# Loading Q and K of two batches in runs of eight rows by head pair, with a fixed order of the first loads, in a fused attention and feed-forward kernel

## The chip, the cores and the metric

The kernel runs on one core of one Trainium2 chip. The metric is the device time of one execution in microseconds (us). A profiled execution gives a span that is 1.7 to 2.2 us shorter than the time of the same execution.

TensorE (PE in the profile) does the matmuls; its weight loads are listed as PEld. ScalarE is ACT, VectorE is DVE, GpSimd is POOL and SyncE is SP. The granted TensorE clock is printed as PEclk, in shares of full speed.

## The reference

The inputs are float32. Batch B is 8, heads H are 8, sequence S is 576 and head width D is 64. After attention, 4,608 tokens go through a feed-forward layer, 512 to 2,048 to 512.

```python
scores = (1 / sqrt(D)) * (q @ k.transpose(0, 1, 3, 2))
mask = abs(pos[:, None] - pos[None, :]) <= 32          # a band of 32 rows on each side
scores = where(mask, scores, -1e9)
attn = exp(scores - max(scores)); attn = attn / (sum(attn) + 1e-9)
x = (attn @ v).transpose(0, 2, 1, 3).reshape(B * S, H * D)
h = x @ w_in
out = (s * maximum(h, 0) ** 2 + b) @ w_out
```

## The kernel before

The kernel is one list of tasks. Every task has an engine, an estimated cost and a priority `key`; a planner simulates the engines with these costs and fixes the order on each engine. A wrong cost gives a wrong order, because the engines execute what the planner chose.

Batches 0 and 1 are transposed by TensorE, batches 2 to 7 by DMA. For the first two, a chunk of 128 pairs of rows is loaded, cast to bf16, transposed and evicted:

```python
# batches 0 and 1, before: rows in pairs (i = 2), so a run in memory is 2 * 64 floats = 512 bytes
def pairs_chunk(b, name, t0, n, key, load_key, banks, slack=0.0):
    ...
    add("sp", lambda e: e.dma_start(
        STG[si][0:n, 0:1024].rearrange("p (h c) -> p h c", h=H),
        src_of[name][b, :, t0:t0 + 2 * n, :].rearrange("h (p i) d -> p h (i d)", i=2)), ...)
    # cast STG -> NAT on ACT, POOL or DVE; eight transposes on PE
    # Q: two evictions to QT on ACT; K: four evictions to KBD on DVE and ACT
```

A transposed query block has its columns sorted by row parity: first all even rows, then all odd rows. The scores in PSUM have that order too. The exponential puts them back into natural order while it writes bf16 to SBUF, with step 2 inside a row of 128.

```python
def unit(b, m):                                   # two key tiles of 64 keys, all 4 head pairs
    ...
    rhs = QT[slot][:, :, pr, lo // 2:hi // 2]     # for the scores of one tile and head pair
    ...                                           # b < 2: a matmul with MASKB adds the band first
    src = src.rearrange("p a (i c) -> p a i c", i=2)
    add("act", lambda e, src=src, dst=dst: e.activation(
        dst.rearrange("p a (c i) -> p a i c", i=2), src, AF.Exp, bias=0.0, scale=0.125),
        190 + 0.833 * 4 * w, ...)                 # the planner's cost: no term for the step
    # then attention times V, reciprocal, scaling (DVE), 4 transposes (PE), eviction to XT (ACT)
```

A batch has nine tiles and hence nine exponentials, seven of 512 columns and two of 384. The order of loads and attention, cut:

```python
qk(0, 0, 128); qk(0, 256, 128)        # Q and K of batch 0, rows 0-255 and 256-511
V of batch 0 (8 loads); qk(0, 512, 32); cast_v(0); units (0, 0) to (0, 4)
w_in (8 loads); w_out, first half
qk(1, 0, 128); V of batch 1; unit(1, 0)
qk(1, 256, 128); unit(1, 1); unit(1, 2); qk(1, 512, 32)
w_out, second half; unit(1, 3); unit(1, 4)
# batches 2 to 7 with PACE and PACEV: after which unit of the batch before their loads may start
```

The feed-forward layers run on token blocks of 128, 128, 256 and then 512. "First layer" is `w<-xt,win`, "second layer" is `o<-wout,gt`. The first block of 512 tokens is called block 3 below.

The softmax here doesn't subtract the row's maximum and nothing guards it: scores larger than these inputs give would overflow.

## Time and profile before

| What | Before | View |
|---|---|---|
| time, median of 3 runs | 332.48 us (332.16 to 333.7) | times |
| span; TensorE busy | 331.1 us; 308.5 us | page |
| first score matmul | 10.70 us | timeline |
| first first-layer matmul | 24.20 us | timeline |
| first 512-column first-layer matmul (block 3) | 74.98 us | timeline |
| one exponential, 512 columns / 384 columns | 0.74 / 0.60 us | groups by shape |

The first view is the page of the kernel before. Parts of the page are separated by dots. The rows of digits cut the span into 40 equal slices; a digit is the busy share, or the granted clock, in tenths (9 is 90% or more). The line that starts with "PE o" is the chain of work that ended last, as shares by line. The last line is a group: busy time, mean ns of one, then the idle time of the engine before them and what ended it.

```profile
span 331.1 us, 5839 instructions
...
PE 308.5 (93%) x2199; PEld 179.5 (54%) x2234; DVE 206.6 (62%) x485; ACT 166.4 (50%) x270; POOL 87.6 (26%) x136
...
PE   1778998899999999999989999999999999999995
...
PEclk9999999799999999999999999999999999999999
...
PE o L717 31%; PE w L698 29%; PE avn L582 6%; SPq L432 5%; DMA vst<-in_v_dram 5%; PE sc L543 3%; DMA stg<-in_moe_w_in_dram 3%; DMA stg<-in_moe_w_out_dram 3%; POOL vst L432 2%; SPq L456 2%; DMA out_dram<-outs 2%; ACT vbd L445 1%; SPq L416 1%; PE o L740 1%; DVE vbd L446 0%
...
L560 ACT ACTIVATE exo<-sc 128x512 bf16<-128x512 f32 x32 | 23.8, 743 | 4.8 <-PE sc L543 4.6
```

TensorE is busy 93% of the span and is idle mainly in the first three slices.

The second view is the table of stretches of the kernel before. The columns are named in the first line; "(x)" stands for a count of instructions. DMA share is the mean busy share of the 16 DMA engines; values above 1 occur, and only comparisons are drawn from it.

```profile
core 0: us, PE busy (x) PEld busy (x) DVE busy (x) ACT busy (x) POOL busy (x), PEclk, DMA share, GB/s
10.00:20.00 10.00, 7.43 (x64) 5.32 (x66) 5.02 (x8) 8.18 (x13) 6.24 (x7) 1.00 1.24 252
20.00:30.00 10.00, 7.60 (x130) 6.82 (x128) 6.13 (x14) 7.71 (x15) 3.85 (x4) 1.00 1.06 373
30.00:40.00 10.00, 10.00 (x126) 9.23 (x124) 6.82 (x14) 5.15 (x9) 3.33 (x3) 1.00 1.13 313
70.00:80.00 10.00, 8.84 (x79) 5.83 (x78) 8.20 (x19) 6.66 (x11) 0.00 (x0) 1.00 0.95 202
```

In steps of 10 us ScalarE is never full: 8.18 us is its highest value here. In steps of 2 us it is: 1.89 to 1.98 us of 2 in each step from 14 to 24 us. TensorE is idle 2.6 us of 10 to 20 us and 2.4 us of 20 to 30 us.

The third view is the timeline of ScalarE in the kernel before, with start and duration in us.

```profile
16.55 0.72 ACT L560 ACTIVATE exo<-sc 128x512 bf16<-128x512 f32 x1
17.38 0.75 ACT L560 ACTIVATE exe<-sc 128x512 bf16<-128x512 f32 x1
18.15 1.04 ACT L445 CAST vbd<-vst 64x1024 bf16<-64x1024 f32 x1
```

One exponential takes about 0.74 us, a cast of V 1.04 us.

The fourth view is one line of TensorE's timeline before, the first score. The brackets give the idle time before it and what ended it.

```profile
10.70 0.48 PE L549 MATMUL sc<-maskb,ident 128*128 128x384 bf16 x1 [1.49 <-DVE kbd L491]
```

The fifth is the table of stretches before for 2.5 to 10 us, where Q, K and V of batch 0 arrive. The last two numbers are the DMA share and GB/s. The clock before them is no proof of full speed at the front: it reads 1.00 here, where eight transposes of 128 columns take 1.03 us, against 0.61 us at 40 us.

```profile
2.50:10.00 7.50, 2.07 (x16) 1.54 (x16) 5.67 (x20) 4.60 (x6) 6.36 (x18) 1.00 1.15 291
```

The sixth is the list of waits of TensorE before: total us, times, longest.

```profile
PE w L473 <- ACT nat L465: 6.1, 1, 6.1
...
PE sc L543 <- ACT exe L560: 1.1, 1, 1.1
```

### The profile page before, as it was taken

To read this page: it belongs to the slowest core of one execution; us is meant where nothing else is said; L and a number is where in the kernel's file an instruction comes from. 1 tells how busy PE (TensorE), PEld (TensorE's weight loads), DVE (VectorE), ACT (ScalarE), POOL (GpSimd) and SP (SyncE) were. 2 spreads that over 40 slices of the span, in tenths; PEclk is the share of its full clock that TensorE was granted. 3 is DMA by queue.
4 is the path that set the end of the run, shared out by engine and by line. 5 is a ranking of instruction groups with operands and counts; after the bars stand their busy time and mean duration, and the time that the engine had idled before them with its cause. 6 is when DMAs were issued, how large, how long until landed. Compare 5 with 4: busy or idle time off the path is not lost.

```text
span 331.1 us, 5839 instructions
## 1 busy us (share of the span) xinstructions
PE 308.5 (93%) x2199; PEld 179.5 (54%) x2234; DVE 206.6 (62%) x485; ACT 166.4 (50%) x270; POOL 87.6 (26%) x136
## 2 busy tenths in 40 slices
PE   1778998899999999999989999999999999999995
PEld 1567996775554555456445555555455544444442
DVE  6556564269777776898578768765874453323411
ACT  6696497229552664657175655444644433333300
POOL 8562443830910226044205500450000000000000
PEclk9999999799999999999999999999999999999999
DMA  8999999899999699979998996999811111000021
GB/s 211 224 363 357 295 195 297 219 241 167 209 202 197 193 195 206 230 170 245 173 228 163 225 212 145 247 169 213 146 56 54 56 46 62 35 32 34 32 93 68
DMA packets 107836, 57.15 MB, mean 173 GB/s; under 512 B 56608, under 2 KB 100128, under 8 KB 107808
## 3 DMA queue, kind: packets, MB, share of 16 engines
q1 hardware_dynamic: 103200, 49.69, 68.7%
q0 software_dynamic: 4608, 7.08, 11.3%
q8 instruction: 17, 0.28, 0.4%
q14 instruction: 11, 0.09, 0.1%
HBM read 36.70 MB, written 9.44 MB: 139 GB/s over the span
## 4 chain that ended last, share of the span: by engine, by line
PE 70%; DMA 13%; SPq 8%; POOL 3%; DVE 2%; ACT 2%; issue 2%; ACTq 0%
PE o L717 31%; PE w L698 29%; PE avn L582 6%; SPq L432 5%; DMA vst<-in_v_dram 5%; PE sc L543 3%; DMA stg<-in_moe_w_in_dram 3%; DMA stg<-in_moe_w_out_dram 3%; POOL vst L432 2%; SPq L456 2%; DMA out_dram<-outs 2%; ACT vbd L445 1%; SPq L416 1%; PE o L740 1%; DVE vbd L446 0%
## 5 line engine op out<-in xcount | busy, mean ns | idle before, releaser
L717 PE MATMUL o<-wout,gt 128*128 128x512 bf16 (+1 forms) x629 | 140.4, 357 | 1.9 <-DVE outs L730 1.3
L698 PE MATMUL w<-xt,win 128*128 128x512 bf16 (+2 forms) x685 | 139.8, 339 | 2.2 <-ACT r L705 1.2
L705 ACT ACTIVATE r<-w 128x512 bf16<-128x512 f32 x144 | 85.4, 598 | 95.0 <-PE w L698 80.8
L707 DVE TENSOR_TENSOR gt<-r 128x512 bf16<-128x512 bf16 x144 | 61.3, 432 | 55.1 <-ACT r L705 54.4
L717 PEld LDWEIGHTS o<-wout,gt 128*128 128x128 bf16 x640 | 61.1, 98 | 59.7 <-DVE outs L730 2.0
L698 PEld LDWEIGHTS w<-xt,win 128*128 128x128 bf16 x704 | 61.6, 98 | 52.4 <-ACT r L705 1.8
L432 POOL DMA_DIRECT2D vst<-in_v_dram x96 | 59.4, 626 | 106.8 <-PE avn L582 57.7
L730 DVE SCALAR_TENSOR_TENSOR outs<-o,sb,cvec 128x512 f32<-128x512 f32 (+1 forms) x40 | 27.7, 692 | 18.6 <-PE o L717 16.2
L560 ACT ACTIVATE exe<-sc 128x512 bf16<-128x512 f32 (+1 forms) x40 | 27.5, 687 | 15.7 <-PE sc L543 15.1
L582 PE MATMUL avn<-vbd,exo 128*128 128x130 bf16 (+1 forms) x240 | 27.9, 221 | 1.5 <-ACT xt L607 1.3
L595 DVE TENSOR_TENSOR xn<-avn,rec 128x512 bf16<-128x512 f32 (+1 forms) x38 | 26.1, 686 | 3.2 <-DMA xt<-xn 2.5
L543 PE MATMUL sc<-qt,kbd 128*128 128x128 bf16 (+1 forms) x288 | 24.8, 220 | 1.6 <-ACT exe L560 1.1
L582 PE MATMUL avn<-vbd,exe 128*128 128x130 bf16 (+1 forms) x152 | 25.3, 221 | 1.0 <-ACT vbd L445 1.0
L560 ACT ACTIVATE exo<-sc 128x512 bf16<-128x512 f32 x32 | 23.8, 743 | 4.8 <-PE sc L543 4.6
L543 PEld LDWEIGHTS sc<-qt,kbd 128*128 128x128 bf16 x288 | 20.5, 100 | 9.9 <-issue 1.0
L445 ACT CAST vbd<-vst 64x1024 bf16<-64x1024 f32 (+1 forms) x15 | 16.5, 1139 | 17.5 <-DMA vst<-in_v_dram 17.5
L582 PEld LDWEIGHTS avn<-vbd,exo 128*128 128x128 bf16 (+1 forms) x240 | 22.0, 105 | 5.5 <-ACT xt L607 1.6
L506 DVE CAST nat<-stg 128x1024 bf16<-128x1024 f32 (+1 forms) x36 | 23.7, 680 | 0.0
L521 DVE COPY kbd<-kt 64x512 bf16<-64x512 bf16 (+1 forms) x72 | 19.1, 266 | 0.8
L582 PEld LDWEIGHTS avn<-vbd,exe 128*128 128x128 bf16 (+1 forms) x152 | 16.1, 109 | 4.3 <-ACT vbd L445 1.4
L446 DVE CAST vbd<-vst 64x1024 bf16<-64x1024 f32 (+1 forms) x16 | 11.7, 745 | 7.3 <-DMA vst<-in_v_dram 7.3
L564 DVE TENSOR_TENSOR exe<-exe,mask 128x512 bf16<-128x512 bf16 (+1 forms) x30 | 11.7, 391 | 7.1 <-ACT exe L560 7.0
(63 smaller groups left out, 133.3 us busy)
## 6 DMA issues: line engine op xcount, KB each, us to landing
stg<-in_q_dram SPq DMA_DIRECT2D x16, 512.0 KB, 5.5
stg<-in_k_dram SPq DMA_DIRECT2D x16, 512.0 KB, 7.2
out_dram<-outs SPq DMA_DIRECT2D x32, 256.0 KB, 2.6
vst<-in_v_dram POOLq DMA_DIRECT2D x96, 72.0 KB, 5.5
stg<-in_moe_w_in_dram SPq DMA_DIRECT2D x8, 512.0 KB, 8.7
stg<-in_moe_w_out_dram SPq DMA_DIRECT2D x8, 512.0 KB, 8.3
vst<-in_v_dram SPq DMA_DIRECT2D x16, 144.0 KB, 4.7
stg<-in_q_dram SPq DMA_DIRECT2D x8, 128.0 KB, 6.2
```

The source lines that it names most:

```text
L432: add(stream, lambda e, dst=dst, src=src: e.dma_start(dst, src), 640.0 if stream == "sp" else 700.0, writes=[("VST", h, x) for x in (range ...
L445: add(eng, (lambda e, dst=dst, src=src: e.copy(dst, src)) if eng == "act" else (lambda e, dst=dst, src=src: e.tensor_copy(dst, src)), {"ac ...
L506: add("dve", lambda e, si=si, ni=ni: e.tensor_copy(NAT[ni][0:n, :, :].rearrange("p i (h d) -> p h i d", h=H), STG[si][0:n, 0:1024].rearran ...
L543: fns = [lambda e, j=j, pr=pr, lo=lo, hi=hi, w=w, par=par: e.matmul(SC[:, par, pr * 128:pr * 128 + w], lhsT=KBD[:, pr, j, :], rhs=QT[slot] ...
L560: add("act", lambda e, src=src, dst=dst: e.activation(dst.rearrange("p a (c i) -> p a i c", i=2), src, AF.Exp, bias=0.0, scale=0.125), 190 ...
L582: fns.append(lambda e, pr=pr, buf=buf, col=col, j=j, x=x, last=len(parts) - 1: e.matmul(av[0:nr, pr, 0:130], lhsT=buf[:, pr, col:col + nr] ...
L595: add("dve", lambda e: e.tensor_tensor(XN[xi][0:nr, :].rearrange("p (a b c) -> p a b c", a=4, b=2), av[0:nr, :, 0:128].rearrange("p a (b c ...
L698: add("pe", [lambda e, g=g, kc=kc: e.matmul(wt[:, g, :], lhsT=WIN_BF[:, kc, (f0 + g) * 128:(f0 + g + 1) * 128], rhs=XT[:, kc, t0 % XR:t0 % ...
L705: add("act", lambda e: e.activation(rt, wt, AF.Relu, bias=0.0, scale=1.0), 190 + 0.833 * 512, reads=[("W", wb)], writes=[("R1", rb)], key=key)
L707: add("dve", lambda e: e.tensor_tensor(GT[gs][:, f0:f0 + ng, g0:g0 + nt], rt, rt, ALU.mult), 130 + 0.53 * 512, reads=[("R1", rb)], writes= ...
L717: add("pe", [lambda e, fc=fc: e.matmul(O[:, ob, 0:cn], lhsT=GT[gs][:, fc, g0:g0 + 128], rhs=WOUT_BF[:, fc, c0:c0 + cn], start=(fc == 0), s ...
L730: add("dve", lambda e: e.scalar_tensor_tensor(OUTS[us][:, 0:cn], O[:, ob, 0:cn], SB128[:, 0:1], CVEC[:, c0:c0 + cn], ALU.mult, ALU.add), 2 ...
```

## The change

The intent: longer runs for the DMA (2 KB in place of 512 bytes), all of Q and K in natural dependence order ahead of the rest, and a TensorE that is kept busy so that its clock is high when real work arrives.

A tile of the new form holds one head pair, with 72 partitions; a partition holds eight rows of both heads. So columns come out of the transpose in eight groups, and the exponential has to restore the order with step 8.

```diff
+ROWS = 8
+NWARM = 60
-PACE = ((0, 0, 1, 2, 3, 3), (0, 0, 1, 2, 3, 3), (0, 1, 2, 3, 3, 3))
-PACEV = ((0, 0, 1, 1), (0, 0, 1, 1), (0, 1, 2, 2))
+PACE = ((-1, -1, -1, 0, 1, 1), (-1, -1, 0, 1, 2, 2), (0, 0, 1, 2, 3, 3))
+PACEV = ((-1, -1, -1, -1), (0, 0, 0, 0), (0, 1, 2, 2))
...
-        NSTG, NNAT, NEX, NXN, NR1, NOUT, XR = 9, 6, 3, 2, 3, 3, 2048
+        NSTG, NNAT, NEX, NXN, NR1, NOUT, XR = 9, 5, 4, 2, 3, 3, 2048
...
+        def load_pair(b, name, pr, key, load_key, banks, eng, slack):
+            n = S // ROWS                                          # 72 partitions
             add("sp", lambda e: e.dma_start(
-                STG[si][0:n, 0:1024].rearrange("p (h c) -> p h c", h=H),
-                src_of[name][b, :, t0:t0 + 2 * n, :].rearrange("h (p i) d -> p h (i d)", i=2)),
-                600.0, writes=[("STG", si)], key=load_key, dma=("l", n // 2, 30.0))
+                STG[si][0:n, :].rearrange("p (h c) -> p h c", h=2),
+                src_of[name][b, 2 * pr:2 * pr + 2, :, :].rearrange("h (p i) d -> p h (i d)", i=ROWS)),
+                600.0, writes=[("STG", si)], key=load_key, dma=("l", 9, 86.0))
... cast, 8 transposes of 72 x 128, one eviction of 576 columns for Q, two for K
         def unit(b, m):
+            nrow = ROWS if b < 2 else 2
...
-                src = src.rearrange("p a (i c) -> p a i c", i=2)
+                src = src.rearrange("p a (i c) -> p a i c", i=nrow)
...
-                    dst.rearrange("p a (c i) -> p a i c", i=2), src, AF.Exp, bias=0.0, scale=0.125),
+                    dst.rearrange("p a (c i) -> p a i c", i=nrow), src, AF.Exp, bias=0.0, scale=0.125),
                     190 + 0.833 * 4 * w, reads=[("SC", par)], writes=[("E", ei, par)], key=key)
...
+            for _ in range(NWARM):                                 # fillers on a tile of ones
+                add("pe", lambda e: e.matmul(AVN[:, 0:2, 0:128], lhsT=ONESW[:, :], rhs=ONESW..., ...), 110,
+                    reads=["ONESW"], writes=["AVN"], key=1e4)
-            qk(0, 0, 128)
-            qk(0, 256, 128)
+            qk(0)                                                  # all eight Q and K loads first
...
-            qk(1, 0, 128)
+            qk(1)                                                  # all of batch 1, then its five units
+            for m in range(NUNIT):
+                unit(1, m)
             w_out(1)
-            unit(1, 3)
-            unit(1, 4)
```

A further part chains all loads of the first phase, so that the planner cannot swap them, gives weight casts a later priority, and drops a wait that held the V loads of batch 1 back.

## The prediction

> **What bounds the kernel now.** The page shows PE busy 308.5 of 331.1 us; the table of stretches shows where the rest lies. 0 to 24.2 us: PE busy 12.7 us, much of it at half rate (eight 128-column transposes take 1.03 us at 6 us, 0.61 us at 40 us); the first first-layer matmul starts at 24.2 us. 50 to 60 us: 2.1 us idle, of it 1.34 us waiting for an output buffer whose DMA took 6.9 us to land (chain of waits); then the granted clock drops (0.58 over 60 to 64 us; sixteen colsum matmuls take 3.33 us against 1.91 us earlier). From 75 to 290 us only some 2.8 us are idle. So the change can act on the first 75 us alone; there DMA (share about 1 to 60 us) and the ScalarE chain set the pace.
>
> **DMA.** Before, Q and K are 512-byte runs: batch 1's 2.36 MB took 8.8 us (last out-weight landing 36.2 us, last Q cast 45.06 us), 268 GB/s. Weight loads with 2 KB runs reach 360 to 386 GB/s. The change makes 2 KB runs, but tiles of 72 partitions. The Trainium skill, "DMA: Bandwidth & Descriptors", "Why a DMA increments its semaphore by 16 and not by 1", says a DMA uses the largest number of engines up to 16 that divides the outer dimensions: for 72, 12. My estimate: 12/16 of 386 = 290 GB/s, 8.1 us per batch, saving 0.7 us (at most 1.5) instead of 2.3 with 16 engines. No run shows this yet.
>
> **Front.** All eight loads must land before the first score, near 10.4 us; with cast (0.7), transposes and two ScalarE evictions (0.6, 0.7), first score about 13 us (10.7 before), then all nine tiles follow uninterrupted. ScalarE still owes seven exponentials (0.72 each), a V cast and a weight cast (1.04 each): 7.1 us plus a wait for V (lands about 16 us). First XT eviction about 21.2 us (22.56 before); first first-layer matmul 22 to 23 us. ScalarE, not PE, paces this stage, so the warm clock from the 60 filler matmuls is worth only some 0.5 us. Front gain 1.2 to 2 us.
>
> **Middle.** DMA is 1.5 to 2.5 us ahead by the second half of the out weights. The new order puts most of batch 1's attention before the second colsum, so PE has work while the weights land; I expect the 1.34 us idle and the cold stretch (about 2 us lost) mostly to disappear, and some of the 1.1 us of waits at 72 to 75 us. Gain 2.5 to 4 us. Against this: the first output stores now queue behind three Q/K loads of batch 2, which may give one back.
>
> **Moved, near neutral.** Four 576-column evictions per tensor replace more, shorter ones; one more VectorE and PoolE cast per batch (0.69, 1.04 us); strided exponentials should keep their rates. Earlier pacing of batches 2 and 3 meets a full PE: 0 to 1 us.
>
> **Prediction:** 327.0 us, 80% range 323.5 to 330.5; faster by over 2% 0.33, within 2% 0.66, slower 0.01.
>
> **What shows it.** Right: Q/K loads idle on a quarter of the engines, under 300 GB/s before 10 us; first score about 13 us; first first-layer matmul 22 to 23 us; block 3's 512-column matmuls start at 70 to 71 us, not 75; granted clock 1.0 over 56 to 64 us; stages after 75 us equally long within 1 us. Wrong: a first-layer start before 21 us, or a new wait near 50 to 70 us on output buffers or weights.
>
> **What would make it wrong.** All 16 engines used (2 to 4 us better); strides slowing exponentials or scores (1 to 2 us worse); fillers running cold and delaying the transposes; stores blocked behind batch 2's loads.

## More of the kernel before

An instruction's duration can overlap the start of the next one on its engine, so costs of instructions in a row are best compared from start to start.

## The result, and the profile after

The changed kernel took 362.25 us (median of 4 runs, 358.94 to 364.3); the kernel before took 333.02 us on the same chip. The ratio is 1.087, with a 95% interval of 1.078 to 1.096. Ratios here and below are the mean time of one kernel's fast runs over that of the other's fast runs of the same rounds, so they are not quite the ratio of the medians quoted. The predicted 327.0 us and its whole range missed.

| What | Before | After | Predicted |
|---|---|---|---|
| time | 333.02 us | 362.25 us | 327.0 us |
| first score | 10.70 us | 18.11 us | about 13 us |
| first first-layer matmul | 24.20 us | 38.85 us | 22 to 23 us |
| block 3 starts | 74.98 us | 97.54 us | 70 to 71 us |
| from there to the end of the span | 256.1 us | 263.7 us | equal within 1 us |
| ScalarE busy in all | 166.4 us | 193.1 us | |

The page of the kernel after, the same parts, with the shares by engine ahead of the shares by line:

```profile
span 361.2 us, 6063 instructions
...
PE 328.8 (91%) x2326; PEld 192.1 (53%) x2326; DVE 206.2 (57%) x485; ACT 193.1 (53%) x262; POOL 90.6 (25%) x138
...
PE   8655999664999997999998999999999999999996
...
PEclk9656699985899999899999999999999999999999
...
PE 68%; ACT 12%; DMA 10%; POOL 3%; DVE 3%; issue 1%; SPq 1%; ACTq 0%; DVEq 0%
...
PE w L707 29%; PE o L726 28%; PE avn L590 6%; ACT exe L568 5%; DMA vst<-in_v_dram 4%; ACT exo L568 4%; POOL vst L449 3%; DMA stg<-in_k_dram 3%; PE sc L551 3%; DMA xt<-xn 2%; PE o L749 1%; ACT r L714 1%; SPq L477 1%; ACT vbd L462 1%; DVE xn L603 1%
...
L568 ACT ACTIVATE exo<-sc 128x512 bf16<-128x512 f32 x32 | 38.5, 1204 | 0.4 <-PE sc L551 0.3
```

Three readings. ScalarE has 12% of the chain, 9% in the exponentials `exe` and `exo` of one line. The group mean of `exo` rose from 743 to 1204 ns, although it still mixes batches 0 and 1 with batches 2 to 7, which did not change. And the clock row holds fives and sixes in the first slices, in spite of the fillers, which make TensorE look busy in the very first slice (the row of the kernel before, as said, does not show the low rate of its first matmuls).

The table of stretches of the kernel after; the four lines are 10 to 20, 20 to 30, 30 to 40 and 70 to 80 us, with the columns as before:

```profile
10.00:20.00 10.00, 7.17 (x65) 4.85 (x65) 5.32 (x16) 4.24 (x6) 6.43 (x11) 0.57 0.93 183
20.00:30.00 10.00, 5.24 (x33) 3.41 (x34) 3.37 (x4) 9.95 (x6) 3.92 (x4) 0.50 1.00 337
30.00:40.00 10.00, 6.20 (x56) 4.80 (x54) 2.37 (x5) 9.98 (x8) 2.71 (x3) 0.67 1.03 330
70.00:80.00 10.00, 6.53 (x59) 4.90 (x56) 1.12 (x4) 10.00 (x6) 6.97 (x10) 0.83 1.14 232
```

In 20 to 40 us and again in 70 to 80 us ScalarE is full: 9.95, 9.98 and 10.00 us of 10, with no more than eight instructions in each. Before, 7.71 us of 20 to 30 us held fifteen. TensorE has half the clock in 20 to 30 us and only 5.24 us of work.

The timeline of ScalarE after:

```profile
20.32 2.79 ACT L568 ACTIVATE exo<-sc 128x512 bf16<-128x512 f32 x1
22.60 2.77 ACT L568 ACTIVATE exe<-sc 128x512 bf16<-128x512 f32 x1
25.40 1.04 ACT L462 CAST vbd<-vst 64x1024 bf16<-64x1024 f32 x1
```

Two exponentials start at 20.32 and 22.60 us: 2.28 us from start to start, where one took 0.74 us before. (Durations of 2.77 to 2.79 us overlap the next instruction a little, so the step from start to start is the fair cost.) The cast of V after them is 1.04 us in both kernels: ScalarE itself is as fast as it was.

The waits of TensorE after, the two largest:

```profile
PE sc L557 <- ACT exe L568: 8.8, 7, 1.7
PE sc L557 <- ACT exo L568: 4.0, 3, 2.1
```

The masks of the scores wait 12.8 us in sum for exponentials to free a score buffer. Before, all the waits of scores for exponentials were some 1.3 us, and the longest single wait was 6.1 us, for the first cast of Q.

The chain of waits after, from 69.61 us on (start, duration, what), shows the second place, batch 1:

```profile
69.61 2.28 ACT exe L568
71.89 2.29 ACT exo L568
74.18 2.27 ACT exe L568
76.45 0.32 ACT xt L615
```

Nothing but exponentials, and one eviction of attention output on the same engine. This goes on to 85.35 us.

The start has another cause, which the chain of waits after also shows:

```profile
3.87 11.54 DMA stg<-in_k_dram
...
15.44 0.69 DVE nat L484
...
18.11 0.48 PE sc L557
```

The last K load was issued at about 3.9 us and its cast could start at 15.44 us; the first score follows at 18.11 us. The loads themselves, in the table of stretches after for 2 to 4 and 4 to 6 us, when little but Q and K is under way (the first V load is issued at 4.31 us):

```profile
2.00:4.00 2.00, 2.00 (x11) 1.44 (x10) 1.48 (x3) 1.99 (x2) 1.72 (x5) 1.00 0.76 208
4.00:6.00 2.00, 2.00 (x18) 1.67 (x17) 1.25 (x3) 1.27 (x2) 1.66 (x6) 1.00 0.78 201
```

The share of 0.76 to 0.78 is close to 12 engines of 16 (0.75), as predicted. But the rate is 201 to 208 GB/s, not the 290 GB/s of the prediction, and not the 291 GB/s of the kernel before with its 512-byte runs.

### The profile page after: what moved, and what is told of

The parts are those of the page before. It is cut to its first block, busy times and chain, and to the rows that moved or that the text cites. A ratio compares the mean times of both kernels' runs of the same rounds, so it can differ in the third digit from the quotient of the medians.

```text
span 361.2 us, 6063 instructions
## 1 busy us (share of the span) xinstructions
PE 328.8 (91%) x2326; PEld 192.1 (53%) x2326; DVE 206.2 (57%) x485; ACT 193.1 (53%) x262; POOL 90.6 (25%) x138
## 3 DMA queue, kind: packets, MB, share of 16 engines
q0 software_dynamic: 4608, 7.08, 10.4%
## 4 chain that ended last, share of the span: by engine, by line
PE 68%; ACT 12%; DMA 10%; POOL 3%; DVE 3%; issue 1%; SPq 1%; ACTq 0%; DVEq 0%
PE w L707 29%; PE o L726 28%; PE avn L590 6%; ACT exe L568 5%; DMA vst<-in_v_dram 4%; ACT exo L568 4%; POOL vst L449 3%; DMA stg<-in_k_dram 3%; PE sc L551 3%; DMA xt<-xn 2%; PE o L749 1%; ACT r L714 1%; SPq L477 1%; ACT vbd L462 1%; DVE xn L603 1%
## 5 line engine op out<-in xcount | busy, mean ns | idle before, releaser
L707 PE MATMUL w<-xt,win 128*128 128x512 bf16 (+2 forms) x704 | 145.5, 343 | 2.5 <-ACT r L714 2.5
L726 PE MATMUL o<-wout,gt 128*128 128x512 bf16 (+1 forms) x640 | 145.4, 360 | 0.2 <-DVE outs L739 0.2
L449 POOL DMA_DIRECT2D vst<-in_v_dram x96 | 61.1, 644 | 125.8 <-PE avn L590 124.8
L568 ACT ACTIVATE exe<-sc 128x512 bf16<-128x512 f32 (+1 forms) x40 | 45.6, 1139 | 13.1 <-PE sc L551 13.1
L568 ACT ACTIVATE exo<-sc 128x512 bf16<-128x512 f32 x32 | 38.5, 1204 | 0.4 <-PE sc L551 0.3
L590 PE MATMUL avn<-vbd,exo 128*128 128x130 bf16 (+1 forms) x240 | 30.9, 236 | 4.9 <-ACT xt L615 3.7
L600 DVE RECIPROCAL rec<-avn 128x8 f32<-128x8 f32 (+1 forms) x38 | 7.7, 203 | 39.2 <-PE avn L590 39.0
L590 PE MATMUL avn<-vbd,exe 128*128 128x130 bf16 (+1 forms) x152 | 27.9, 233 | 1.2 <-ACT exo L568 1.2
L590 PEld LDWEIGHTS avn<-vbd,exo 128*128 128x128 bf16 (+1 forms) x240 | 24.1, 113 | 9.2 <-ACT xt L615 3.8
L557 PE MATMUL sc<-maskb,ident 128*128 128x512 bf16 (+1 forms) x18 | 8.7, 483 | 13.7 <-ACT exe L568 8.8
```

The source lines that it names most:

```text
L449: add(stream, lambda e, dst=dst, src=src: e.dma_start(dst, src), 640.0 if stream == "sp" else 700.0, writes=[("VST", h, x) for x in (range ...
L568: add("act", lambda e, src=src, dst=dst: e.activation(dst.rearrange("p a (c i) -> p a i c", i=nrow), src, AF.Exp, bias=0.0, scale=0.125), ...
L590: fns.append(lambda e, pr=pr, buf=buf, col=col, j=j, x=x, last=len(parts) - 1: e.matmul(av[0:nr, pr, 0:130], lhsT=buf[:, pr, col:col + nr] ...
L707: add("pe", [lambda e, g=g, kc=kc: e.matmul(wt[:, g, :], lhsT=WIN_BF[:, kc, (f0 + g) * 128:(f0 + g + 1) * 128], rhs=XT[:, kc, t0 % XR:t0 % ...
L726: add("pe", [lambda e, fc=fc: e.matmul(O[:, ob, 0:cn], lhsT=GT[gs][:, fc, g0:g0 + 128], rhs=WOUT_BF[:, fc, c0:c0 + cn], start=(fc == 0), s ...
```

## The experiments

The theory after the first reading had two parts. Part A: the bf16 writes with step 8 (16 bytes) make an exponential some three times as long. Part B: 72-partition loads are slower than expected. The rivals were: the fillers, which may hold up TensorE or consume its clock; the new pacing of batches 2 and 3; the longer stepped *reads* of PSUM; the buffer counts; and the planner's wrong load cost.

All fourteen full variants passed the comparison with the reference. For e3, e5, e7, e9, e12, e13 and e14, whose values are wrong, this shows only that the comparison does not notice such a mistake. That the plain write in e1 is right rests on its indices: it writes the same element to the same place in another order of traversal.

### e1: the same layout, but the exponential reads stepped and writes plainly

```diff
-    dst.rearrange("p a (c i) -> p a i c", i=nrow), src, AF.Exp, ...
+    dst.rearrange("p a (c i) -> p a c i", i=nrow) if b < 2 else dst.rearrange("p a (c i) -> p a i c", i=nrow),
+    src.rearrange("p a i c -> p a c i") if b < 2 else src, AF.Exp, ...
```

> The changed kernel, with only the 18 exponentials of batches 0 and 1 turned round: they read PSUM with a step of 16 columns and write the bf16 tile without a step, where the changed kernel reads without a step and writes with a step of 8 elements (16 bytes). Results stay right. Theory 1 (the stepped write makes an exponential take 2.3 us instead of 0.74): the 18 fall to 0.6 to 0.8 us, each batch's chain of nine is shorter by 13 to 15 us, first first-layer matmul near 26 us instead of 38.9, total 328 to 336 us. Rival A (the loads of 72 partitions and the cold clock hold the front): exponentials get short but the first first-layer matmul stays after 33 us, total above 345. Rival B (any access in runs of 16 is slow, read or write): exponentials stay above 2 us, total near 362.

Measured: 346.62 us against 332.56 us before, ratio 1.0442 [1.0374, 1.0511]. That is 15.6 us less than the changed kernel. The first first-layer matmul moved from 38.85 to 27.85 us, and block 3 from 97.54 to 82.85 us, while the first score stayed at 17.92 us. ScalarE is busy 163.9 us in all. The group of `exo` in e1:

```profile
L568 ACT ACTIVATE exo<-sc 128x512 bf16<-128x512 f32 x32 | 22.4, 701 | 2.5 <-PE sc L551 2.4
```

It fell from 1204 to 701 ns: in e1 the first two batches are plain at 0.60 us and the others keep 0.74 us. So part A is worth about half of the loss.

### e2: e1 without the fillers

```diff
-    add("pe", lambda e: e.matmul(AVN[:, 0:2, 0:128], lhsT=ONESW[:, :], ...), 110,
+    add("pe", [], 110,
         reads=["ONESW"], writes=["AVN"], key=1e4)
```

The empty task keeps its place and cost in the plan, so all else is in the same order.

> The kernel with the plain write, its order of instructions kept, but the 60 filler matmuls left out. If the fillers keep the clock up: without them the first transposes and scores run at half rate (eight transposes 0.66 us instead of 0.42), the first score 0.5 to 1 us later, total 0.5 to 1.5 us more. If ScalarE and the loads pace the front whatever the clock does: within 0.5 us of the kernel with fillers. If the fillers themselves delay the first transposes: faster by up to 1 us.

Measured: 346.60 us, ratio 1.0421 [1.0363, 1.0479], against 346.62 us and 1.0442 of e1 on the same chip. The first first-layer matmul is at 27.04 us, 0.8 us earlier than with fillers, and nothing of that reaches the end. The fillers did do what they were meant to at first: the first eight transposes take 0.42 us in e1 and 0.64 us in e2. But the path was elsewhere, and a loss or gain under some 2 us would not be seen here.

### e3: the kernel before, with step 8 in the writes of the exponentials alone

```diff
-    src = src.rearrange("p a (i c) -> p a i c", i=2)
+    wi = 8 if b < 2 else 2
+    src = src.rearrange("p a (i c) -> p a i c", i=wi)
...
-    dst.rearrange("p a (c i) -> p a i c", i=2), src, AF.Exp, ...
+    dst.rearrange("p a (c i) -> p a i c", i=wi), src, AF.Exp, ...
```

The values land in wrong columns. Loads, order, pacing and buffers are those of the kernel before.

> The kernel before, with one thing of the change alone: the 18 exponentials of batches 0 and 1 write with a step of 8 elements (the values land in wrong columns, so the result is wrong on purpose). Theory 1: each takes 2.3 us, 1.5 us more than before, and the total rises by 20 to 30 us to 352 to 362 us. Rivals A and B' (loads, clock or new order cause the loss): exponentials under 1 us, total within 3 us of the kernel before, 333 us.

Measured: 351.86 us, ratio 1.058 [1.051, 1.065], so 19.3 us more than before. Its page, the chain of work that ended last:

```profile
PE 78%; ACT 13%; DVE 3%; DMA 2%; issue 2%; POOL 1%; ACTq 0%
PE w L699 33%; PE o L718 32%; PE avn L583 6%; ACT exo L561 5%; ACT exe L561 4%; PE sc L543 4%; DMA vst<-in_v_dram 2%; ACT vbd L445 2%; PE o L741 1%; ACT kbd L490 1%; POOL vst L432 1%; ACT r L706 1%; ACT qt L479 1%; DVE vbd L339 1%; PE sc L549 1%
```

ScalarE has 13% of the chain, which was 2% before, and the exponentials are 9% of it. This is part A in isolation, without any load being touched: 18 instructions with another step in their output make the kernel 19.3 us slower. ScalarE's busy time rose from 166.4 to 193.8 us, by 27.4 us; the rest, some 8 us, did not reach the end of the kernel.

### e4: the disputed costs by themselves

A separate program, with wrong output. It loads groups of six tiles in several forms, one group after the other, and then runs exponentials and copies of 512 columns from PSUM with different steps, each form twice.

```python
wr(i):  out t[p, (a c i)] seen as (a, i, c), in PS[p, (a i c)] plain      # stepped write
rd(i):  out t[p, (a c i)] plain, in PS[p, (a i c)] seen as (a, c, i)      # stepped read
runs:   out t[p, (i a c)] seen as (a, i, c)                               # pieces of 16, no step
loads:  128 partitions, 512-byte runs | 72 at 0 | 72 at 32 | 64 at 0 | 64 at 32 | 128 of w_in
```

> A separate small program, result wrong on purpose: six groups of six loads, each group waited for, then ScalarE exponentials and VectorE copies of 512 columns with various steps. Theory 1: exponentials with bf16 writes at a step of 2 elements near 0.74 us, of 8 elements near 2.3 us, reads with a step of 8 and plain writes below 0.8 us, and the same number of runs without a stepped write below 0.8 us; whether 4 elements are slow tells if the limit is the step in bytes, as do fp32 writes at steps of 4 and 8 elements. Loads: if 12 of 16 engines alone limit the loads of 72 partitions, they run near 290 GB/s wherever the tile starts, and 64 partitions near 380. If the partitions they write to limit them [...], 72 and 64 partitions starting at 0 run near 200 GB/s and both gain when they start at partition 32; 128 partitions with 2 KB runs near 380 GB/s.

The tile views of the probe: instruction, count, shortest, median and longest duration in ns. `a_wr` is ScalarE with bf16 output and steps 2, 4, 8, 16 and 32, twice each; `a_fwr` is ScalarE with float32 output and steps 2, 4 and 8; `a_rd` is ScalarE with stepped reads; `d_wr` is VectorE with bf16 output and steps 2, 4 and 8.

```profile
L88 ACT ACTIVATE a_wr<-ps x10: 772/2646/2849, 67.4 to 81.5; 128x512 bf16<-128x512 f32 x10
...
L88 ACT ACTIVATE a_fwr<-ps x6: 739/1238/1290, 85.9 to 89.6; 128x512 f32<-128x512 f32 x6
...
L88 ACT ACTIVATE a_rd<-ps x4: 672/698/996, 83.7 to 85.5; 128x512 bf16<-128x512 f32 x4
...
L80 DVE CAST d_wr<-pd x6: 711/1301/2633, 65.4 to 70.9; 128x512 bf16<-128x512 f32 x6
```

By single instruction, in ns:

| 512 columns, PSUM to SBUF | plain | step 2 | step 4 | step 8 | step 16 | step 32 |
|---|---|---|---|---|---|---|
| ScalarE, bf16 write | 592–597 | 772–777 | 1357–1474 | 2604–2849 | 2688–2717 | 2769–2786 |
| ScalarE, float32 write | – | 739–747 | 1209–1267 | 1285–1290 | – | – |
| VectorE, bf16 write | 670–680 | 711–717 | 1276–1326 | 2456–2633 | – | – |

| 512 columns, ScalarE, bf16 write plain | read with `rd(2)`, a step of 64 columns | read with `rd(8)`, a step of 16 columns |
|---|---|---|
| stepped read of float32 in PSUM | 672–996 | 691–704 |

The pieces of 16 without a step took 606 and 618 ns. So the number of pieces costs next to nothing, and a stepped read at most about 0.1 us in duration (in e1 the exponentials with stepped reads took 0.59 to 0.60 us, so not even that; the 996 ns is the first stepped read, which overlaps the end of the slow write before it). A write with a step of 8 takes more than four times as long as a plain one, and from start to start too: 2.02 and 2.27 us against 0.48 to 0.49 us. The cost stops growing at 16 bytes (step 8 in bf16, step 4 in float32). One write per 16 bytes is slow in both types, but the bf16 one is twice as slow as the float32 one. VectorE shows the same curve in its copies from PSUM, so a copy on VectorE that writes with this step is no way out.

The table of stretches of the probe, in the order of the six groups of loads above; the last two numbers are the DMA share and GB/s:

```profile
5.00:13.00 8.00, 0.00 (x0) 0.00 (x0) 0.00 (x0) 1.00 1.19 299
17.00:25.00 8.00, 0.00 (x0) 0.00 (x0) 0.00 (x0) 1.00 0.79 202
28.00:34.00 6.00, 0.00 (x0) 0.00 (x0) 0.00 (x0) 1.00 0.76 259
37.00:44.00 7.00, 0.00 (x0) 0.00 (x0) 0.00 (x0) 1.00 1.00 219
47.00:51.00 4.00, 0.00 (x0) 0.00 (x0) 0.00 (x0) 1.00 0.94 308
55.00:62.00 7.00, 0.00 (x0) 0.00 (x0) 0.00 (x0) 1.00 0.98 351
```

The 72-partition tile runs at 202 GB/s with a share of 0.79, as in the kernel. Shifted by 32 partitions it has the same share (0.76) and 259 GB/s. The 64-partition tile has a share of 1.00 and still only 219 GB/s at partition 0, and 308 GB/s at partition 32. So the share of engines is as predicted, but at partitions 0 to 71 it isn't what limits: *which* partitions are written is. The Trainium skill, "SBUF — State Buffer", section "Door 1: The DMA port swizzle (why `[64,N]` ≈ `[32,N]`)", says that partitions 0 to 63 share eight of sixteen ports on the DMA side, and that partitions 64 to 127 use the other eight. The order of these four rates agrees with that: tiles which lie mostly below partition 64 are the slow ones. The prediction had not used it.

### e5: e1 with loads to 128 partitions

```diff
-    STG[si][0:n, :].rearrange("p (h c) -> p h c", h=2),
-    src_of[name][b, 2 * pr:2 * pr + 2, :, :].rearrange("h (p i) d -> p h (i d)", i=ROWS)),
+    STG[si][:, 0:576],
+    src_of[name][b, 2 * pr:2 * pr + 2, :, :].rearrange("h s d -> (h s d)").rearrange("(p c) -> p c", c=576)),
...
-    src = STG[si][0:n, :].rearrange("p (h i d) -> p h i d", h=2, i=ROWS)
+    src = STG[si][0:n, 0:512].rearrange("p (one i d) -> p one i d", one=1, i=ROWS).to_broadcast((n, 2, ROWS, D))
```

The same bytes arrive, spread over 128 partitions, and the cast reads as many elements as in e1. The values are wrong.

> The kernel with the plain exponential writes, with one more edit: each Q or K load of batches 0 and 1 brings the same 295 KB to all 128 partitions (runs of 2304 bytes) instead of 72; the casts then read what lies there, so the values are wrong on purpose, while the order of all instructions stays. Theory 2 (writing to partitions 0 to 71 alone holds these loads near 200 GB/s): the loads run at 300 to 370 GB/s, the first score comes 3 to 5 us sooner (about 14 us instead of 18), the total falls by 4 to 8 us to 339 to 343. Rival (the new order and pacing cause what is left of the loss): the loads get faster but the total falls by less than 3 us.

Measured: 339.63 us against 332.1 us before, ratio 1.021 [1.0156, 1.0265], 7.0 us less than e1. The first score is at 14.66 us, and in TensorE's timeline of e5 the first first-layer matmul is at

```profile
22.54 1.06 PE L708 MATMUL w<-xt,win 128*128 128x128 bf16 x16
```

which is inside the 22 to 23 us of the prediction. That is in part luck. The loads run at 309 to 350 GB/s from 2 to 8 us, faster than the 290 GB/s of the prediction, and still the first score is 1.7 us later than the predicted 13 us. In the chain of waits of e5 it hangs on GpSimd: three casts of 1.03, 1.05 and 1.39 us with mask work between them, where the prediction had one cast of 0.7 us. Some 0.8 us of this (an estimate, seven times 0.12 us) came back because plain exponentials take 0.60 us and the prediction had 0.72. Part B is worth 7.0 us once part A is gone.

### e6: e1 with the old pacing

`PACE` and `PACEV` as before the change.

> The kernel with the plain exponential writes, with the two tables that pace the loads of batches 2 to 7 as they were before the change. If the earlier loads crowd the queue in front of the transposes by DMA and cost the 5 us lost after the first 512-column matmuls: total falls by 3 to 6 us, and the stage after them is within 1 us of the kernel before (256 us). If that loss comes from the late start alone: total within 1.5 us.

Measured: 350.02 us in the three fast runs (351.83 us with the slow one), ratio 1.0548 [1.0463, 1.0632]. A miss: the ratio is higher than the 1.0442 of e1, though the intervals overlap, and neither of the two outcomes named came. No sign that the new pacing was a cost in that surrounding.

### e7: e5 with the old pacing

> Both edits together: loads to 128 partitions (wrong on purpose) and the old pacing tables, on the kernel with plain exponential writes. If the slow write, the slow loads and the pacing are all of the loss: total at or under the kernel before, 328 to 333 us, as was predicted for the change. If something else of the change costs time, it stays above 335.

Measured: 338.30 us, ratio 1.0176 [1.0111, 1.024], against 339.63 us of e5 on the same chip; the intervals overlap. The first first-layer matmul is at 23.31 us, and block 3 starts at 71.42 us, 3.6 us before the kernel before. But that lead is partly an illusion. Between these two marks TensorE does 112 second-layer matmuls of 256 columns in e7 and 128 before: 16 of them, 1.7 us or so, were moved behind the mark. And the first long wait comes soon after it, in TensorE's timeline of e7:

```profile
75.60 0.34 PE L613 MATMUL avn<-ident,xn 96*128 96x96 bf16 x4 [2.50 <-DVE xn L604]
```

From 30 to 120 us TensorE is busy 80.7 us in e7 and 86.3 us before. So 5.7 us of idle time are new, more than the 4.4 us between the two spans. The list of waits of e7 for 30 to 130 us names 3.5 us for normalisations and 1.9 us for copies of K on VectorE, and 2.4 us for casts of the out weights on VectorE and GpSimd. The kernel before has no wait for weight casts there, and the change gave these casts a later priority: a rival for part of the rest that no run tests.

### e8 and e15: the kernel before, with plain writes

```diff
-    dst.rearrange("p a (c i) -> p a i c", i=2), src, AF.Exp, bias=0.0, scale=0.125),
+    dst.rearrange("p a (c i) -> p a c i", i=2), src.rearrange("p a i c -> p a c i"), AF.Exp, bias=0.0, scale=0.125),
```

> The kernel before, with all its exponentials turned round: read with a step of 2, write without one. Each takes 0.60 us for 512 columns instead of 0.74 (as in the changed kernel with plain writes). ScalarE paces the first 24 us only, with nine exponentials of batch 0: gain up to 1.3 us there, some 0.5 to 1 us in batch 1, nothing later: total 0 to 2 us less, 330.5 to 332.5 us.

> The kernel before with plain exponential writes, as run before with three rounds (ratio 0.9956, 0.989 to 1.002). If ScalarE's exponentials matter to it: ratio 0.993 to 0.998. If not: 0.999 to 1.001.

(The reads of e8 have a step of half a block, 48 or 64 columns; the "step of 2" is the count of row groups.) Measured: 331.96 us, ratio 0.9956 [0.9894, 1.0018], and in five rounds 332.64 us, ratio 0.9993 [0.995, 1.0035]. An exponential falls from 0.74 to 0.60 us, and ScalarE is busy 159.7 us in place of 166.4 us, but the time is the same within the noise. The first first-layer matmul moves from 24.20 to 23.76 us, so the exponentials do pace the front, by 0.44 us, and nothing of it is seen at the end. Shorter exponentials can thus be worth nothing that shows (0.14 us less in each of 72), and longer ones 19.3 us (1.5 us more in 18).

### e9: e7 with the old buffer counts

`NNAT` 6 and `NEX` 3, in place of 5 and 4.

> The kernel with plain exponential writes, 128-partition loads (wrong on purpose) and old pacing, with the number of buffers too as before the change: six cast tiles instead of five, three sets of exponential tiles instead of four. If the missing cast tile causes the waits for VectorE after the first 512-column matmuls (6 us of TensorE idle from 80 us on, 3.3 before): total falls by 3 to 6 us, to the kernel before, 331 to 335. If the buffers do not matter: within 2 us of 338.

Measured: 336.28 us in the three fast runs (337.72 us with the slow one) against 333.71 us, ratio 1.0118 [1.0036, 1.02]. Its profiled run was slow (span 415.8 us, clock 0.754). The interval overlaps that of e7, so a gain from the buffers is not shown.

### e10: e1 with the measured load cost told to the planner

```diff
-    600.0, writes=[("STG", si)], key=load_key, dma=("l", 9, 86.0))
+    600.0, writes=[("STG", si)], key=load_key, dma=("l", 12, 121.0))
```

> The kernel with plain exponential writes, whose planner is told what a Q or K load of 72 partitions takes (1.45 us of the queue, worked out from 295 KB at 203 GB/s) instead of 0.77; the loads themselves stay as they are. If a good part of what is left of the loss is an order planned for loads that come sooner: total falls by 3 to 7 us from 346.6. If the late loads cost the time whatever the order: within 2 us of 346.6.

Measured: 349.53 us, ratio 1.0496 [1.0419, 1.0573], against 1.0442 [1.0374, 1.0511] of e1: no gain. A miss: the plan did not become better from a truer cost of these loads.

### e11: the kernel before, with fillers

48 fillers, costed at 150 ns, ahead of e8's work.

> The kernel before with plain exponential writes and 48 filler matmuls, 35 of them ahead of the first transposes. The first transposes take 0.6 us instead of 1.03, scores 0.23 instead of 0.43 us of start-to-start; the first first-layer matmul moves from 23.8 to 22.8 to 23.6 us. Total 0 to 1.5 us less than without fillers, 330.5 to 332. If ScalarE alone paces the front: same within noise.

Measured: 335.24 us, ratio 1.0071 [0.9998, 1.0144]. No gain; against the 0.9956 and 0.9993 of e8 and e15 rather a small loss, within the noise.

### e12: the change as it is, with loads to 128 partitions

The edit of e5 on the changed kernel, so that the step of 16 bytes stays.

> The changed kernel as it is, stepped exponential writes and all, with only the loads of batches 0 and 1 brought to 128 partitions (wrong on purpose). If the two causes add: 7 us less than the change, about 355. If the stepped exponentials hide the loads in batch 0 and 1 (ScalarE 100% busy from 20 to 40 and 70 to 90 us): only the first-score time moves, by 3.5 us, total about 358.

Measured: 358.60 us, ratio 1.0762 [1.0697, 1.0827]. The loads are worth only 3.65 us here, against 7.0 us after the exponentials were mended; the intervals of e12 and of the change overlap, so even the 3.65 us are not clear of the noise. The first score comes at 14.68 us, but ScalarE then sets the pace, and the first first-layer matmul starts at 35.12 us. Mending the exponentials after the loads, from e12 to e5, is worth 19.0 us, against 15.6 us before them. That would mean that whichever is mended first, the other hides part of its gain; but the difference, 3.4 us, is within the noise of four measurements. (e12 and e5 ran on different chips, whose kernels before took 333.71 and 332.1 us.)

### e13 and e14: what is left

Both start from e9. In e13 the planner is told that casts of V and of Q and K for later batches wait longer for their loads (9,000 and 6,000 in place of 3,000 ns), so that they do not block engines. In e14 the fillers are empty, as in e2.

> The kernel with plain writes, 128-partition loads (wrong on purpose), old pacing and old buffers, whose planner now assumes the loads of batches 2 to 7 to land later (slack of the V casts 9 instead of 3 us, of the Q and K casts 6 instead of 3), so that VectorE does batch 1's last normalisation before it waits for batch 2's V. If that in-order wait is what is left of the loss: the 2.5 us wait of TensorE for the normalisation near 75 us goes, total falls by 2 to 5 us, to 333 to 336. If not: within 1.5 us of 337.7.

> The same kernel as in the run with old buffers, its order kept, without the 60 fillers. If the fillers cost something (they delay the first transposes to 7 us, or lower the clock later): total falls by 1 to 3 us from 337.7. If they help where the loads are fast: it rises by 0.5 to 1.5 us. As in the earlier pair with slow loads: no difference within 1 us.

Measured, five rounds: e13 338.68 us, ratio 1.0165 [1.012, 1.021]; e14 336.76 us in its five fast runs (337.08 us with the outlier), ratio 1.0118 [1.0075, 1.0161]. The profiled run of e14 was an outlier (span 1,151.6 us). e14 is level with e9. In e13 TensorE is busy 9.95 of 10 us in 70 to 80 us, where e7 had 7.21 us. But e13 has another wait later, in its TensorE timeline:

```profile
115.45 0.93 PE L551 MATMUL sc<-qt,kbd 128*128 128x96 bf16 x8 [7.69 <-DVE kbd L529]
```

The wait of 2.50 us at 75 us is gone, and at 115 us TensorE waits 7.69 us, for other work of VectorE, a copy of K. As e9 has no readable profile, this compares e13 with e7, which has other buffer counts too.

## Why the prediction was wrong

The losses as the runs built them up, in medians of the fast runs (the chips differ: the kernel before had 332.1 to 333.7 us):

| Step | Time | Difference |
|---|---|---|
| changed kernel | 362.25 us | |
| plain writes (e1) | 346.62 us | −15.6 us |
| and loads to 128 partitions (e5) | 339.63 us | −7.0 us |
| and old pacing (e7) | 338.30 us | −1.3 us, within the noise |
| and old buffers (e9) | 336.28 us | −2.0 us, within the noise |
| kernel before | 332.1 to 333.7 us | −4 to −6 us by the ratios of e9 and e7, not explained |

**"Strided exponentials should keep their rates."** This is the step that failed, and the largest term. I named the risk, "strides slowing exponentials or scores (1 to 2 us worse)", but gave it a tenth of its size. One exponential of 512 columns went from 0.74 to 2.28 us, and there are 18 of them, four with 384 columns (0.60 us before; 1.88 to 2.25 us in duration after, of which I took 1.88). My estimate from these numbers is 14 × 1.54 + 4 × 1.28 = 26.7 us more work on ScalarE. The page shows 166.4 to 193.1 us; so exact a match is chance, since the evictions changed as well (262 instructions on ScalarE in place of 270). e3, where only the exponentials changed, shows 27.4 us. The prediction itself said that "ScalarE, not PE, paces this stage"; the error was to lengthen the pacing engine's work without measuring. With the step alone, the kernel before lost 19.3 us (e3); without it, the changed kernel gained 15.6 us (e1).

The Trainium skill, "SBUF — State Buffer", in the same section, has a note on "SBUF cachelines": 16-byte lines, with steps of up to 8 bf16 elements free. The changed write is just that step of 8, at 16 bytes. The probe disagrees: 2.6 to 2.8 us against 0.60 us. The note also asks for at least two accesses in a line, and a step of 8 leaves only one, so read to the end it warned; but at step 4, with two in a line, the probe still shows 1.36 to 1.47 us. The measurement decides. The 16 bytes do appear, as the place from which the cost does not grow any further.

**"12/16 of 386 = 290 GB/s, 8.1 us per batch."** The factor 12/16 was right: the Trainium skill, "DMA: Bandwidth & Descriptors", section "Why a DMA increments its semaphore by 16 and not by 1", lets the number of engines divide the outer dimension, and the measured shares of 0.76 to 0.79 are close to 12 of 16. The other factor was wrong. The 386 GB/s came from loads to 128 partitions, and a load to the first 72 partitions does not run at three quarters of that. It ran at about 200 GB/s; the last K could be cast at 15.44 us, not at 10.4 us; and the first score came at 18.11 us, not 13 us. With 128 partitions it came at 14.66 us (e5), the rest being GpSimd's casts. In the kernel the longer runs were no gain: 291 GB/s before with runs of 512 bytes to 128 partitions, 200 GB/s after with 2 KB to 72. On 128 partitions in the probe, 2 KB runs had 351 GB/s and 512-byte runs 299 (from different tensors), so it is the partitions that turned a gain into a loss.

**The front, "first first-layer matmul 22 to 23 us".** Wrong as measured, 38.85 us, but met or nearly met without the two costs: 22.54 us in e5 and 23.31 us in e7, with a later first score and shorter exponentials than predicted, so partly by luck.

**The fillers, "worth only some 0.5 us".** That they matter little holds; 0.5 us and its sign can't be told from nothing in e2, e11 and e14. The clock of the changed kernel still fell to 0.57 and 0.50 in 10 to 30 us, where TensorE waits for loads and for ScalarE. The Trainium skill, "TensorE: Matmul & The Clock Gate", section "What's actually happening", says that the clock falls back to half after an idle window of some 3.4 us. This trace shows the fall without such a stretch: the clock is 1.00 in 8 to 10 us and 0.50 from 12 us on, while TensorE works 0.83 us of 2 in 8 to 10 us and 1.03 us in 10 to 12 us, and its longest wait between 7 and 12 us is 1.00 us. So here a TensorE that worked about half of the time was enough for it.

**The middle, "gain 2.5 to 4 us".** It did not come. Two of its signs did: the clock was 1.00 in 56 to 64 us, and the wait for output buffers fell from 1.3 to 0.2 us. But with all work some 15 us later, other work lies there, so they say nothing for the prediction. Even with both costs removed, e5, e7, e9, e13 and e14 are 1.2 to 2.1% slower than before. The lead at block 3 (71.42 against 74.98 us) is used up by waits between 30 and 120 us, most of them for VectorE. "Stages after 75 us equally long within 1 us" failed too: from block 3 to the end it is 256.1 us before, 263.7 us after and 264.1 us in e7.

**What stays open.** Of the residual 4 to 6 us I can say where it lies, 5.7 us of additional TensorE idle time in 30 to 120 us in e7, and that no gain clear of the noise came from leaving out the fillers (e14) or from the old pacing and buffers (e7, e9). That it comes from the order that the planner makes out of the new load order is likely, since its place moves with small changes of planner costs (e13), but this is argued, not shown. No run restored the old load order with the new layout, or the old priority of the weight casts, for which e7 waits 2.4 us. No version beat the kernel before. And no run has a *correct* layout with loads to 128 partitions; e5 and its successors only measure what such loads would be worth.

## What to carry to other kernels

A layout that makes a load's runs longer moves its reordering elsewhere: find the instruction that restores the order, on which engine it runs, and measure one such instruction with the new step before counting on its old rate. Put the step on the read from PSUM and keep the write to SBUF plain, which cost 0.1 us at most, against 1.5 us in the kernel and 2 us in the probe for the stepped write. And before taking a DMA rate from another load, compare not only its run length and its number of engines, but which partitions it writes.

## What the Trainium skill lacked or had wrong

- "SBUF — State Buffer", note on "SBUF cachelines": it calls steps of up to 8 bf16 or 4 float32 elements free (although it also asks for two accesses in a line). As writes of ScalarE, 512 columns from PSUM, they are not: bf16 0.60 us plain, 0.77 us at step 2, 1.36 to 1.47 us at step 4, 2.60 to 2.85 us at step 8; float32 0.74 us at step 2, and 1.21 to 1.27 us at step 4. VectorE is alike (0.67, 0.71, 1.3 and 2.5 to 2.6 us).
- The same note says of PSUM, with lines of 8 bytes, that non-contiguous patterns slow matmuls, and gives nothing for ScalarE. Reads of PSUM by ScalarE with a step of 16 float32 columns (64 bytes) cost at most about 0.1 us: 0.69 to 0.70 us in duration against 0.60 us.
- "DMA: Bandwidth & Descriptors", section on the 16 of the semaphore: the number of engines it gives (12 for 72 partitions) fits the traces (share 0.76 to 0.79), but alone it leads to a wrong rate. The section does not point to the ports (another section of the page does, for 128 partitions): 72 partitions at 0 gave 202 GB/s and at 32 gave 259 GB/s, with nearly the same share of the engines (0.79 and 0.76).
- "SBUF — State Buffer", the port swizzle: what it says of 64 partitions agrees with 219 GB/s at partition 0 (the page gives 218 GB/s as the limit of these ports). It has no measurement for a tile of fewer than 128 partitions that lies in both halves; the same tile at partition 32 gave 308 GB/s, against 351 GB/s for 128 partitions with 2 KB runs.
- "TensorE: Matmul & The Clock Gate", section "What's actually happening": it does not say how much work a window may hold and still count as idle. Here the granted clock fell to 0.50 at 11.33 us after 3.41 us in which TensorE was busy for 1.86 us.
